# New priorities for the projections of the first attention pass, and a new table of scheduling rules, in a fused attention and token-MLP kernel

## The chip, the core and the metric

The kernel runs on one core of a Trainium2 chip. The metric is the device time of one execution in microseconds (us). The engines are PE (TensorE: matmuls; PEld is its weight load), DVE (VectorE), ACT (ScalarE), POOL (GpSimd) and SP (SyncE, which issues the DMAs).

## The reference

Two branches read the same normalised input, and the result joins them. B is 1, S is 2048, D is 640, there are 32 heads of 20, and F is 1536.

```python
xn = layernorm(x)                                   # over D
# A: attention
q, k, v = split_heads(xn @ wqkv)                    # 32 heads of 20
p = softmax(q @ k.T * 20**-0.5)                     # 2048 x 2048 for each head
s = merge_heads(p @ v) @ wo
# B: an MLP over the tokens
h = layernorm(xn)
u = gelu(einsum("bsd,sf->bdf", h, w1) + b1)         # tanh form
y = einsum("bdf,fs->bds", u, w2) + b2               # back to b, s, d
out = x + s * silu(y)
```

## The kernel before

**Units.** The heads are taken in eight groups G of four, and each group in passes of 512 queries. A pass has sixteen chunks of 128 keys. A *unit* is one chunk for one head and 512 queries: a PSUM bank of 128x512 scores. There are 2048 of them. A score matmul (line L1283) has 20 rows of real depth in a tile of 32 rows, so the four heads of a group run side by side in the array. The probabilities go into PV matmuls (L1381) that put the four heads side by side in columns, into one PSUM bank (bank 6), with a column of ones in V that sums the denominator. At the end of a pass (`ep_steps`) DVE transposes, divides and sends the result to DRAM.

**Two ways to an exponential.** ACT takes a *score group* of two or three PSUM banks (the groups are banks 0 to 2 and 3 to 5) and writes bf16 probabilities to `pt_sb` (L1313), a ring of 20 slots of 512. A slot is free again once its PV is done, and a group that doesn't fit at the ring's end starts over at slot 0. DVE instead makes an exponential out of bits: one operation writes the score as an integer that reads as a bf16 (L1324), and three operations on four units at a time (L1362) write copies of it that are shifted in the exponent's bits. PV adds the four versions, with V scaled for each (`vs_sb`, L766). So a DVE unit costs four PV matmuls where an ACT unit costs one. The scheduler lends DVE the third bank of an ACT group, and ACT then takes two.

**Other work.** The layer norm is on DVE and POOL. The first 512 rows of xn are transposed on PE, the others by DMA (`xTd_steps`, from `regC` to `xnT_sb`). For group 0, `qk_steps` makes q and k: five matmuls for 512 or 256 columns (L633), then one copy out of PSUM (by ACT at L1113/L1116, by DVE at L1114/L1117), scaled for q. `v_steps` with half 0 makes V of the first two groups, two chunks at a time: ten matmuls (L746), one copy. The projections of the later groups, the MLP (L648; L656 where a row of the array is used on its own) and the output projection (L965, L970) are cut into jobs that PE takes between the scores.

**The order.** No order is written out by hand. While the program is built, `schedule` plays the engines forward with costs of its own and fixes the order of each engine's instructions; on the chip each engine runs its list in order and waits on semaphores. The parts that the change touches are:

- Jobs that need a PSUM bank stand in `bankq`. During the *ramp* (until the tags in `RAMPEND` are done), `activate_` gives the next free bank (of 3, 4, 5 and 7 at first) to the job with the least of (time its first input is there, but not less than now + `KLEAD`; priority; place). Later it is the first that is due. A job holds its bank until its copy out of PSUM is done. During the ramp ACT and DVE both copy out; after it only DVE does.
- Priorities: 17 and 22.4 for the halves of q of the first block, `KPRIO` + block for keys, `VPRIO` + block for V, `QPRIO` for the second to fourth query blocks. A smaller number goes first. The scores of a pass need the query block of that pass (`qk0_0_1` is the second) and the chunk's keys (`qk0_1_3` is the last second half); PV needs the chunk's V.
- `pe_cands` offers PE the next score group, PV groups or a job's matmul, by ACT's deadline: the time at which ACT runs out of scores. If nothing is ready, and PE's recent activity is low, it sends a *filler* of four matmuls that add zeros into bank 6 (L1398; at the very start L1408). `SLACK`, `MINJ`, `ROOM`, `JOBF`, `LATE`, `PARTS`, `FGAP` are its thresholds. `LATE` is in passes, as are the due times.
- `do_st` decides whether DVE is lent a bank: `LEND` is the amount of work in DVE's queue above which it is not, `DRIDE` and `LONE` rule the extra bank 7. `D_GUARD` is the number of ACT units that must remain in a pass for DVE to take a chunk of it. `TOPP` and `EVP` are the priorities on DVE of the shifted copies and of copies out of PSUM.
- `MLP_A` and `MLP_B` spread the MLP's due times between these two passes. `OPM` is the number of 128-row blocks whose last 128 output columns share one bank and one product on DVE.
- `tune` is called every `WIN` = 16 claimed units and sets the options in `OPTS` to the values that one string of `PLAN` names, a digit for each option. `PLAN` is empty, so every option keeps its one value.

Of the kernel before, what the change touches and what calls it, by code (L numbers as in the profile page):

```python
# [265 lines left out]
class _Kern:  # L266
# [13 lines left out]
    AK = (1.0, 0.83984375, 0.70703125, 0.59375)  # L280
    MEAN4 = 4.159829600672171
    LOG2E = 1.4426950408889634
    D_GUARD = 16
    MLP_A, MLP_B = 2.6, 24.0
    QK_LEAD = 6.0
    SLACK, MINJ = 0.0, 640.0
    ROOM = 6
    ROWM, ROWP, ROWN = 5, 2, 400
    lastrow = None
    MERGE = False  # L290
    OPM = 2
    KLEAD = 300.0
    KPRIO = 22.4
    RAMPEND = ('qk0_1_3', 'qk0_0_1')
    RLEND = 0
    DRDY = 'xn15'
    OPR = 20.0
    QPRIO = (26.5, 29.0, 29.0)
    PVR = False
    JOBF = 4  # L300
    LONE, DLEAD, DRIDE = False, 0.0, 400.0
    NQS = 3
    CONFL = True
    FILL, FGAP, FACT = True, 0.0, 0.6
    LATE = 1.0
    LEND, LEND_MIN = 1800.0, 3
    SHARE = True
    VPRIO = 25.0
# [4 lines left out]
    QC = ((0.5, 3.0), (3.2, 6.4), (9.0, 13.5), (14.0, 18.0), (19.0, 22.0))  # L313
    WIN = 16
    DON = True
    TOPP, EVP = 38.0, 36.0
    GROT = 1
    OPTS = (
        ("SLACK", (120.0, 40.0, 200.0, 320.0)),
        ("MINJ", (640.0, 320.0, 1000.0)),  # L320
        ("ROOM", (3, 6, 0)),
        ("DRIDE", (400.0, 150.0, 700.0)),
        ("LEND", (1800.0, 1300.0, 2400.0, 700.0, 0.0)),
        ("PARTS", ((2,), (2, 1), (3, 1), (1,), ())),
        ("LATE", (2.0, -9.0, 99.0)),
        ("DON", (True, False)),
        ("LONE", (False, True)),
        ("CONFL", (True, False)),
        ("TOPP", (38.0, 22.0)),
        ("EVP", (24.0, 36.0)),  # L330
        ("FGAP", (40.0, 150.0)),
        ("GROT", (1, 0)),
    )
    PLAN = ()
    PARTS = (3, 1)
    DX = (1, 2, 3)
    V1A, V1B = 0.5, 4.0
# [73 lines left out]
    def schedule(self):  # L411
# [82 lines left out]
        def small(fn):  # L494
            def f(e):
# [6 lines left out]
               name="tl", cost=1400.0)  # L502
# [6 lines left out]
                name="id1", cost=300)  # L509
# [70 lines left out]
        def xtag(gb):  # L580
            return tuple(f"xTd{b}" for b in range(4 * gb, 4 * gb + 4)) if gb in DX else tuple(f"xT{gb}{h}_{d}" for h in ("a", "") for d in (0, 2, 4))
# [147 lines left out]
                     f"wp0_{w}", 430.0),  # L729
                    ("tag", f"wp0_{w}")]  # L730

        def v_steps(b, half):
            def make(bk):
                steps = []
                c0, n = (0, 160) if half == 0 else (160, 480)
                bl = [b] if half else [b, b + 1]
                for i, bb in enumerate(bl):
                    rd = [S_("wv")] + ([S_(f"xTb{bb}")] if bb // 4 in DX else [
                        S_(f"xT{dc}_0{'a' if bb < 2 else ''}") for dc in range(5)])
                    for dc in range(5):  # L740
# [5 lines left out]
                        steps.append(("pe", lambda e, dc=dc, i=i, bb=bb: e.matmul(  # L746
                            ps(bk, n, i * n), xnT_sb[:, dc, bb * 128:(bb + 1) * 128], wv_sb[:, dc, c0:c0 + n],
                            start=(dc == 0), stop=(dc == 4)), rd, [bank_slot[bk]], f"v{half}_{bb}", mm(n)))
# [271 lines left out]
        bankq = []  # L1020
# [6 lines left out]
            jobs.append(_Job(name, make if callable(make) else (lambda bk, m=make: m), requires, False, prio, at))  # L1027

        def add_bank_job(name, make, requires=(), prio=50.0, at=0.0):
            bankq.append(_Job(name, make, requires, True, prio, at))  # L1030

        def release(j):
            if j.bk is not None:
# [38 lines left out]
        def activate_():  # L1072
# [5 lines left out]
            while changed:  # L1078
# [493 lines left out]
        for gb in range(4):  # L1572
            if gb in DX:
                for b in range(4 * gb, 4 * gb + 4):
                    add_job(f"xTd{b}", xTd_steps(b), (f"xn{b}",), 22.0)
            xt = xtag(gb)
            if gb == 0:
                for h in (0, 1):
                    hp = "" if h else "a"
                    for dcs in ((0, 1), (2, 3), (4,)):  # L1580
                        add_bank_job(f"xT{h}_{dcs[0]}", xT_steps(h, dcs), (f"xn{2 * h}", f"xn{2 * h + 1}"), 18.0 + h)
                    xh = tuple(f"xT0{hp}_{d}" for d in (0, 2, 4))
                    add_bank_job(f"q0_0{hp}", qk_steps(0, 0, 256 * h, 256, hp), (f"xT0{hp}_0", "wp0_0"), 17.0 if h == 0 else 22.4)
# [24 lines left out]
        for G in range(1, NG):  # L1608
            cs = sorted({(80 * G - 80) // 128, (80 * G - 1) // 128})
            for w in (1, 0):  # L1610
# [5 lines left out]
                    at=(4 * G - 1.0 if G < NG - 1 else 24.0))  # L1616
# [484 lines left out]
        while True:  # L2101
# [84 lines left out]
```

## Time and profile before

| What | Value |
|---|---|
| Time, median of 3 runs | 753.57 us (753.44 to 754.69) |
| The profiled execution's own time | 754.1 us |
| Its span, first to last instruction | 752.3 us |
| Busy: PE, DVE, ACT | 716.3, 719.0, 730.0 us |
| Mean granted PE clock | 0.999 |
| Exps on ACT | 681 instructions, 1552 units |
| Exps on DVE | 496 units, 372 shifted copies |
| Filler matmuls (L1398) | 244 |
| DMA | 42.66 MB, 57 GB/s on the mean |

A line of the groups reads: source line, engine, operation, output <- inputs, shapes, count, then busy time and the mean duration of one in ns, then the idle time of the engine just before such instructions and what ended most of it. Durations of one engine's neighbours overlap, so the pace is read from the starts. A line of a timeline has the start and the duration in us, the operation, the count of merged instructions, and in brackets the idle time before it and its releaser. A line of the waits has the total, the number of times and the longest, in us.

### The profile page before, as it was taken

How to read it: one execution, taken by the hardware profiler on the slowest of the kernel's cores; microseconds unless marked ns; L12 is line 12 of the kernel's file. 1: busy time of each engine (PE TensorE's matmuls, PEld its weight loads, DVE VectorE, ACT ScalarE, POOL GpSimd, SP SyncE). 2: the span in 40 equal slices, each digit the busy share in tenths (PEclk: the TensorE clock that was granted, in tenths of full speed). 3: DMA queues.
4: the chain of work that ended last, by engine and by line, in shares of the span. 5: the costliest groups of instructions: out<-in, count | busy, mean ns of one | idle time of the engine just before them, and what ended most of it. 6: DMA issues, size and time to landing. Idle time of an engine off the chain costs nothing.

```text
span 752.3 us, 23672 instructions
## 1 busy us (share of the span) xinstructions
PE 716.3 (95%) x10561; PEld 243.6 (32%) x10561; DVE 719.0 (96%) x1320; ACT 730.0 (97%) x707; POOL 15.3 (2%) x23
## 2 busy tenths in 40 slices
PE   9899999999999999999999999999999999999997
PEld 7332222222233232323223332323233332333233
DVE  7889999999999999999999999999999999999996
ACT  5989999999999999999999999999999999999995
POOL 4200000000000000000000000000000000000000
PEclk9999999999999999999999999999999999999999
DMA  8754111110121031212111131301325501041102
GB/s 237 155 110 48 56 38 37 20 38 5 38 62 20 13 76 31 72 24 69 20 38 21 30 87 24 74 13 29 79 76 81 128 28 51 7 152 47 47 15 70
DMA packets 119738, 42.66 MB, mean 57 GB/s; under 512 B 79172, under 2 KB 118468, under 8 KB 119588
## 3 DMA queue, kind: packets, MB, share of 16 engines
q1 hardware_dynamic: 119636, 41.15, 23.4%
q8 instruction: 82, 1.34, 0.8%
q14 instruction: 20, 0.16, 0.1%
HBM read 26.37 MB, written 10.22 MB: 49 GB/s over the span
## 4 chain that ended last, share of the span: by engine, by line
ACT 76%; PE 18%; DVE 6%; issue 0%; DVEq 0%
ACT pt_sb L1313 74%; PE ps_all L1381 5%; PE ps_all L1283 5%; PE ps_all L648 5%; DVE dt_sb L1324 1%; PE ps_all L1408 1%; ACT zt_sb L849 1%; DVE dt_sb L1362 1%; ACT zt_sb L844 1%; DVE bst_sb L532 1%; DVE bst_sb L530 1%; DVE regC L548 1%; PE ps_all L965 1%; PE ps_all L633 0%; DVE v_sb L1114 0%; PE ps_all L746 0%
## 5 line engine op out<-in xcount | busy, mean ns | idle before, releaser
L1313 ACT ACTIVATE pt_sb<-ps_all 128x1024 bf16<-128x1024 f32 (+1 forms) x681 | 711.2, 1242 | 4.9 <-PE ps_all L1283 2.1
L1324 DVE TENSOR_SCALAR dt_sb<-ps_all 128x512 uint16<-128x512 f32 x496 | 328.4, 683 | 15.9 <-PE ps_all L1283 8.9
L1283 PE MATMUL ps_all<-qk_sb 32*128 32x512 bf16 (+1 forms) x2128 | 269.1, 376 | 26.4 <-ACT pt_sb L1313 22.9
L1362 DVE TENSOR_SCALAR dt_sb<-dt_sb 128x2048 uint16<-128x2048 uint16 x372 | 241.2, 689 | 1.5
L1283 PEld LDWEIGHTS ps_all<-qk_sb 32*128 32x128 bf16 x2128 | 68.4, 91 | 280.9 <-ACT pt_sb L1313 226.4
L1381 PE MATMUL ps_all<-dt_sb,vs_sb 128*21 128x512 bf16 (+1 forms) x1536 | 130.7, 376 | 0.9 <-DVE dt_sb L1362 0.5
L1381 PE MATMUL ps_all<-pt_sb,v_sb 128*21 128x512 bf16 (+1 forms) x1616 | 127.0, 374 | 1.9 <-DVE v_sb L1114 0.9
L648 PE MATMUL ps_all<-regC,regA 128*32 128x128 bf16 (+1 forms) x1472 | 65.5, 297 | 0.0
L648 PE MATMUL ps_all<-regB,regA 128*32 128x128 bf16 (+1 forms) x1480 | 65.2, 298 | 0.3 <-DVE qs_sb L698 0.3
L1381 PEld LDWEIGHTS ps_all<-dt_sb,vs_sb 128*21 128x21 bf16 x1536 | 33.4, 90 | 51.7 <-issue 31.2
L1381 PE MATMUL ps_all<-dt_sb,v_sb 128*21 128x512 bf16 (+1 forms) x512 | 49.2, 377 | 0.1
L1381 PEld LDWEIGHTS ps_all<-pt_sb,v_sb 128*21 128x21 bf16 x1616 | 30.9, 90 | 49.2 <-issue 35.9
L648 PE MATMUL ps_all<-xnT_sb,wqk_sb 128*32 128x512 bf16 x640 | 46.1, 382 | 0.0
L648 PEld LDWEIGHTS ps_all<-regB,regA 128*32 128x32 bf16 x1480 | 27.4, 96 | 23.3 <-issue 10.9
L648 PEld LDWEIGHTS ps_all<-regC,regA 128*32 128x32 bf16 x1472 | 27.8, 96 | 22.0 <-issue 10.6
L965 PE MATMUL ps_all<-wv_sb,xnT_sb 128*128 128x512 bf16 (+1 forms) x160 | 27.3, 301 | 0.0
L656 PE MATMUL ps_all<-regC,regA 32*128 32x512 bf16 x64 | 24.6, 384 | 0.0
L648 PE MATMUL ps_all<-wv_sb,xnT_sb 128*32 128x480 bf16 x320 | 22.1, 369 | 0.3 <-DVE qs_sb L1117 0.3
L1505 DVE STREAM_TRANSPOSE tr_sb<-ps_all 128x512 f32<-128x512 f32 x31 | 22.0, 711 | 0.0
L656 PE MATMUL ps_all<-regB,regA 32*128 32x512 bf16 x56 | 21.5, 384 | 0.0
L1381 PEld LDWEIGHTS ps_all<-dt_sb,v_sb 128*21 128x21 bf16 x512 | 13.0, 90 | 20.6 <-issue 14.2
L1398 PE MATMUL ps_all<-wp_sb,zw_sb 128*21 128x512 bf16 (+1 forms) x244 | 19.4, 373 | 0.0
(88 smaller groups left out, 348.5 us busy)
## 6 DMA issues: line engine op xcount, KB each, us to landing
regA<-in_B_w_dram SPq DMA_DIRECT2D x6, 1024.0 KB
regA<-in_B_w_dram SPq DMA_DIRECT2D x8, 768.0 KB
qk_sb<-qk_scratch_dram SPq DMA_DIRECT2D x56, 80.0 KB
qk_scratch_dram<-qs_sb SPq DMA_DIRECT2D x32, 128.0 KB
regA<-in_A_x_dram SPq DMA_DIRECT2D x6, 640.0 KB
ok_scratch_dram<-on_sb SPq DMA_DIRECT2D x96, 20.0 KB
out_dram<-regC SPq DMA_DIRECT2D x3, 640.0 KB
wqk_sb<-in_A_wqkv_dram SPq DMA_DIRECT2D x2, 480.0 KB
```

The lines of the kernel that those rows point to most:

```text
L530: steps.append(("dve", lambda e, b=b: e.bn_stats(bst_sb[:, b, 0:6], regA[:, b, 0:320]), [sx], [s0], f"{nm}s0", 393.0))
L532: steps.append(("dve", lambda e, b=b: e.bn_stats(bst_sb[:, b, 6:12], regA[:, b, 320:640]), [sx], [s1], f"{nm}s1", 393.0))
L648: fns.append(lambda e, c=c, e_=e_: e.matmul(oc(c, e_), lhsT[:, c:e_], rhs, start=start, stop=stop, tile_position=(0, c)))
L656: row = lambda g: (lambda e: e.matmul(oc(0, 128), lhsT[32 * g:32 * g + 32, :], rhs[32 * g:32 * g + 32, :], start=False, stop=False, tile_p ...
L965: steps.append(("pe", lambda e, c=c: e.matmul(ap, oT_sb[:, c, b * 128:(b + 1) * 128], wo_ap[:, c, c0:c0 + n], start=(opens and c == 0), st ...
L1283: t = pr.pe(lambda e, outp=outp, lhsT=lhsT, rhs=rhs, g=g: e.matmul(outp, lhsT, rhs, start=True, stop=True, tile_position=(32 * g, 0)), rea ...
L1313: tk = pr.act(lambda e: e.activation(outp, inp, AF.Exp, scale=math.log(2.0) / 128.0), reads=[bank_slot[b] for b in banks[:n]], writes=[S_( ...
L1324: tk = pr.dve(lambda e: e.tensor_scalar(w, src, WOFF, 0.0, ALU.add, ALU.max), reads=[bank_slot[bk]], writes=[S_(f"dt{d['tl'][0]}_{g}")], n ...
L1362: tk = pr.dve(lambda e: e.tensor_scalar(dst, src, dk, None, ALU.add), reads=[S_(f"dt{b}_{g}") for b in inb for g in range(4)], writes=[S_( ...
L1381: pr.pe(lambda e: e.matmul(outp, lhsT, rhs, start=(k == 0), stop=last, tile_position=(0, 32 * g)), reads=reads, writes=[bank_slot[AB]], na ...
L1398: pr.pe(lambda e, outp=outp, rhs=rhs, g=g: e.matmul(outp, zw_sb[:, 0:DH + 1], rhs, start=False, stop=False, tile_position=(0, 32 * g)), re ...
L1505: steps.append(("dve", lambda e: e.transpose(tr_sb[:, :], ps(AB)), [bank_slot[AB]], [S_("tr")], f"epT{q}", 632.0))
```

## The change

The jobs of the first pass that use a bank can get a priority of their own by name (`JP`). The V jobs are made from a list of groups (`VGRP`), which may have other sizes than two. The ramp ends without waiting for the second query block. Several fixed values change: `D_GUARD`, `MLP_B`, `OPM`, `KLEAD`, `LONE`, `DRIDE`, `LATE`, `EVP`. The options get some more values, `JOBF` becomes one of them, and `PLAN` has 128 strings, one for each 16 units; the first is applied before the first instruction is placed.

```diff
-    D_GUARD = 16
-    MLP_A, MLP_B = 2.6, 24.0
+    D_GUARD = 12
+    MLP_A, MLP_B = 2.6, 21.0
...
-    OPM = 2
-    KLEAD = 300.0
+    OPM = 4
+    KLEAD = 450.0
     KPRIO = 22.4
-    RAMPEND = ('qk0_1_3', 'qk0_0_1')
+    JP = {'q0_0': 26.0, 'k0_1a': 31.14, 'k0_2': 27.02, 'v0_11': 18.6, 'v0_3': 24.18, 'v0_10': 31.03, 'v0_13': 22.04, 'k0_0': 30.89, 'v0_0': 23.13}
+    VGRP = ((0, 2), (2, 2), (4, 2), (6, 2), (8, 2), (10, 2), (12, 2), (14, 2))
+    RAMPEND = ('qk0_1_3',)
...
-    LONE, DLEAD, DRIDE = False, 0.0, 400.0
+    LONE, DLEAD, DRIDE = True, 0.0, 250.0
...
-    LATE = 1.0
+    LATE = 2.0
...
-    TOPP, EVP = 38.0, 36.0
+    TOPP, EVP = 38.0, 18.0
...
     OPTS = (
-        ("SLACK", (120.0, 40.0, 200.0, 320.0)),
+        ("SLACK", (0.0, 120.0, 40.0, 200.0, 320.0)),
...
-        ("PARTS", ((2,), (2, 1), (3, 1), (1,), ())),
-        ("LATE", (2.0, -9.0, 99.0)),
+        ("PARTS", ((3, 1), (2,), (2, 1), (1,), ())),
+        ("LATE", (1.0, 2.0, -9.0, 99.0)),
...
-        ("EVP", (24.0, 36.0)),
-        ("FGAP", (40.0, 150.0)),
+        ("EVP", (36.0, 24.0)),
+        ("FGAP", (0.0, 40.0, 150.0)),
         ("GROT", (1, 0)),
+        ("JOBF", (4, 0, 8)),
     )
-    PLAN = ()
+    PLAN = (
+        "000000000000000", "000000000000000", "000000000000000", "000000000000000", "000000000000000", "200000000000000",
+        "000030000010000", "000000000000000", "000000000000000", "000000000000000", "000000000000000", "020000000000000",
...
+    )
...
-        def v_steps(b, half):
+        def v_steps(b, half, nb=2):
...
-                bl = [b] if half else [b, b + 1]
+                bl = [b] if half else list(range(b, b + nb))
...
-            bankq.append(_Job(name, make, requires, True, prio, at))
+            bankq.append(_Job(name, make, requires, True, self.JP.get(name, prio), at))
...
-            for b in range(4 * gb, 4 * gb + 4, 2):
-                add_bank_job(f"v0_{b}", v_steps(b, 0), xt + ((f"qk0_1_{gb}",) if gb else ("qk0_0_0", "qk0_1_0")), self.VPRIO + gb)
+            for b, nb in self.VGRP:
+                if (b + nb - 1) // 4 == gb:
+                    need = xt + (xtag(gb - 1) if b // 4 < gb else ())
+                    add_bank_job(f"v0_{b}", v_steps(b, 0, nb), need + ((f"qk0_1_{gb}",) if gb else ("qk0_0_0", "qk0_1_0")), self.VPRIO + gb)
```

More of the change, by code (lines that the diff above doesn't have):

```diff
@@ L315 @@
     DON = True
-    TOPP, EVP = 38.0, 36.0
+    TOPP, EVP = 38.0, 18.0
     GROT = 1
     OPTS = (
-        ("SLACK", (120.0, 40.0, 200.0, 320.0)),
+        ("SLACK", (0.0, 120.0, 40.0, 200.0, 320.0)),
         ("MINJ", (640.0, 320.0, 1000.0)),
-        ("ROOM", (3, 6, 0)),
+        ("ROOM", (6, 3, 0)),
         ("DRIDE", (400.0, 150.0, 700.0)),
         ("LEND", (1800.0, 1300.0, 2400.0, 700.0, 0.0)),
-        ("PARTS", ((2,), (2, 1), (3, 1), (1,), ())),
-        ("LATE", (2.0, -9.0, 99.0)),
+        ("PARTS", ((3, 1), (2,), (2, 1), (1,), ())),
+        ("LATE", (1.0, 2.0, -9.0, 99.0)),
         ("DON", (True, False)),
@@ L329 @@
         ("TOPP", (38.0, 22.0)),
-        ("EVP", (24.0, 36.0)),
-        ("FGAP", (40.0, 150.0)),
+        ("EVP", (36.0, 24.0)),
+        ("FGAP", (0.0, 40.0, 150.0)),
         ("GROT", (1, 0)),
+        ("JOBF", (4, 0, 8)),
     )
-    PLAN = ()
+    PLAN = (
+        "000000000000000", "000000000000000", "000000000000000", "000000000000000", "000000000000000", "200000000000000",
+        "000030000010000", "000000000000000", "000000000000000", "000000000000000", "000000000000000", "020000000000000",
+        "200000000000000", "000000000000002", "000000000000000", "010000000010000", "400000000000000", "000000000000000",
+        "001000000000001", "000000000000000", "000020000000000", "020000000000000", "200000000000000", "000000000000201",
+        "400000000000000", "010000000010000", "000004000000000", "000020000000000", "200000000000000", "000000000000000",
+        "000000000000000", "000000000000000", "000000000000000", "010000000010000", "000000000000000", "000000000000000",
+        "000030000010000", "020000000000000", "020004000000000", "010000000000000", "220020000000000", "000004000000000",
+        "000000000000000", "000000000000000", "010000000000000", "000030000010000", "000000000001000", "400000000000000",
+        "000020000000000", "200000000000000", "000000000000000", "000030000010000", "000030000000000", "000000000000000",
+        "000020000000000", "000000000000000", "000004000000200", "000020000000000", "010010000000000", "010010000000000",
+        "000102000010000", "000000000000000", "000020000000000", "000020000000000", "002000000000000", "001001000000000",
+        "020000000000000", "000000000000000", "000000000000000", "000000000000001", "000020000000000", "000020000000000",
+        "000000000000000", "000001000001000", "000000000000000", "000020000000000", "010000000010000", "000000000000000",
+        "010000000010000", "000020000000000", "000030000010000", "000000000000000", "200000000000000", "010004000010000",
+        "000000000000000", "000000000000000", "000000000000000", "000000000000000", "200000000000000", "200000000000000",
+        "000000000000000", "000000000000000", "000000000000000", "000010000000000", "000002000000000", "000000000000000",
+        "000000000000000", "000020000000000", "000004000000000", "000004000000000", "200000000000000", "000004000000000",
+        "000004000000000", "100000000000000", "000030000010000", "000030000010000", "000000000010000", "000004000000000",
+        "000030010000000", "000000000000000", "000004000000000", "000024000000000", "010000000010000", "000000000000000",
+        "000000000000000", "300000000010000", "000004000000000", "020000000000000", "010000000010000", "000000000000000",
+        "000000000000000", "000000000000200", "000030000010000", "010034000000000", "200000000000000", "000004000000000",
+        "000000000000000", "000030000010000",
+    )
```

## The prediction

> **What bounds the kernel now.** I read the page's shares first, then the groups by form, the chain of work, and the timelines of ACT and PE. From the page:
>
> ```profile
> span 752.3 us, 23672 instructions
> PE 716.3 (95%) x10561; PEld 243.6 (32%) x10561; DVE 719.0 (96%) x1320; ACT 730.0 (97%) x707; POOL 15.3 (2%) x23
> ACT 76%; PE 18%; DVE 6%; issue 0%; DVEq 0%
> ```
>
> Three engines are over 95% busy, but three quarters of the chain is ACT. The groups by form say with what:
>
> ```profile
> L1313 ACT ACTIVATE pt_sb<-ps_all 128x1024 bf16<-128x1024 f32 x491 | 481.3, 1127 | 0.9 <-PE ps_all L1283 0.5
> L1313 ACT ACTIVATE pt_sb<-ps_all 128x1536 bf16<-128x1536 f32 x190 | 285.9, 1541 | 4.0 <-PE ps_all L1381 1.9 <-PE ps_all L1283 1.7
> L1324 DVE TENSOR_SCALAR dt_sb<-ps_all 128x512 uint16<-128x512 f32 x496 | 328.4, 683 | 15.9 <-PE ps_all L1283 8.9 <-PE ps_all L656 5.7
> L1362 DVE TENSOR_SCALAR dt_sb<-dt_sb 128x2048 uint16<-128x2048 uint16 x372 | 241.2, 689 | 1.5
> L1398 PE MATMUL ps_all<-wp_sb,zw_sb 128*21 128x512 bf16 x224 | 18.5, 382 | 0.0
> ```
>
> All 2048 score units are here: 491×2 + 190×3 = 1552 on ACT and 496 on DVE. The mean of 1127 ns is not a pace, since successive exps overlap: in the timeline most start 0.904 us apart (two banks) or 1.331 us (three), the fourteen tanh 1.16 us. So ACT's own work is 491×0.904 + 190×1.331 + 14×1.16 = 713.0 us. The first exp starts at 12.09 us, the last ends at 743.59: 731.5 us. Of the 18.5 us between, 1.5 are projections copied out by ACT; 17.0 us are waiting. The starts put 5.4 us of it before 42 us and 11.6 us after. Of the 11.6, 6.9 us are 31 waits of over 0.1 us, scattered from 70 to 726 us, the rest small change. Most of that hides in the overlap and never shows in the idle column. What lies outside the exps is 12.1 us ahead and 8.7 us behind.
>
> The ramp's waiting is in ACT's timeline:
>
> ```profile
> 14.73 2.79 ACT L1313 ACTIVATE pt_sb<-ps_all 128x1536 bf16<-128x1536 f32 x2 [0.78 <-PE ps_all L1283]
> ...
> 21.30 6.82 ACT L1313 ACTIVATE pt_sb<-ps_all 128x1536 bf16<-128x1536 f32 x5 [0.49 <-PE ps_all L1283]
> 28.33 8.18 ACT L1313 ACTIVATE pt_sb<-ps_all 128x1536 bf16<-128x1536 f32 x6 [0.20 <-PE ps_all L1283]
> 37.46 0.60 ACT L1116 ACTIVATE qk_sb<-ps_all 128x512 bf16<-128x512 f32 x1 [0.95 <-PE ps_all L633]
> ```
>
> Sixteen exps of three units pass; then ACT waits 0.95 us for the second query block and 1.93 us more. All engines' timeline shows what for:
>
> ```profile
> 38.11 0.87 PE L746 MATMUL ps_all<-wv_sb,xnT_sb 128*128 128x160 bf16 x10 [0.69 <-ACT qk_sb L1116]
> 38.91 0.40 PE L1398 MATMUL ps_all<-wp_sb,zw_sb 128*21 128x512 bf16 x4
> 39.02 0.49 DVE L1114 CAST v_sb<-ps_all 128x320 bf16<-128x320 f32 x1
> 39.56 0.61 PE L1381 MATMUL ps_all<-pt_sb,v_sb 128*21 128x512 bf16 x8 [0.26 <-DVE v_sb L1114]
> 39.99 9.81 ACT L1313 ACTIVATE pt_sb<-ps_all 128x1536 bf16<-128x1536 f32 x9 [1.93 <-PE ps_all L1381]
> ```
>
> The scores of exp 17 were ready (L1283 at 35.22 us). It waited for room in `pt_sb`, whose 20 slots hold six groups of three. A group leaves by PV (L1381), which lacked V; V's matmul lacked the bank that the query block held until ACT had copied it out. So the first pass ends on: query block, bank, V, PV, exp.
>
> **The change part by part.**
>
> *Projections of the first pass.* The instruction order of the changed kernel puts the second query block (five matmuls of 512) five score groups earlier, ahead of the last three key halves, with DVE copying it out. Three V blocks stand between key halves, where there were two. `VGRP` has the old pairs, and `v0_3`, `v0_11`, `v0_13` name no job: these move nothing. The early q costs PE 5×0.216 = 1.1 us, and the fills of 33 to 35 us (three groups, 0.65 us) show where it goes; if that cover is missing, one key half is 1.1 us later. On DVE the copy (0.60 us) stands behind the layer norm and ahead of a key's; the scores of those keys wait behind it. ACT copies six q/k blocks of 256 (0.33 us each) instead of four and one of 512 (0.55): 0.1 us more.
>
> ACT after: twelve exps run on from 21.3 us, 12×1.331 = 16.0, with the 0.37 us that stands before 28.33, then one key copy of 0.33 us: exp 18 at 38.0 us. Before it was 39.99 + 1.33 = 41.3. Gain 3.3 us if nothing new is late; 2.4 if the key copy waits as the q copy did (0.95); 1.4 if the PV wait (1.93) returns, which is the bound against it. I take 2.6, nearer to the free case: in the order, the PV that exp 17 lacked now stands ahead of score group 18 instead of behind it, and its V no longer behind the query block's bank. All three engines begin the steady part that much earlier, since DVE's first exp (42.57 us) waits for the same end of the ramp.
>
> *Units.* DVE gets 492 instead of 496, ACT 490 exps of two and 192 of three. ACT: −0.904 + 2×1.331 = **+1.8 us**, all on the bounding engine. DVE drops 4×0.60 + 3×0.60 = 4.2 us, which is not the bound.
>
> *The table.* Every sixteen units it sets when DVE is lent a bank, how far PE runs into ACT's deadline, and how many copies PV takes. The first string also overrides the new values of `LONE`, `DRIDE`, `LATE` and `EVP` with the old ones, so those edits move nothing. The table adds no instruction; its whole effect is on the 11.6 us. Evidence from the order: filler groups of four (L1398) fall from 61 to 39; in the first 128 units from 15 to 11, so 18 of the 22 go later. A filler is sent only when PE has nothing else, so PE is starved some 18×0.22 = 4 us less. Against it, PE changes between tilings 1306 times for 1292 (a run of eight PV takes 0.54 us after scores, 0.43 without a change, so 0.11 each: +1.5 us). From below, the gain cannot pass the 6.9 us of waits over 0.1 us; from the other side, the denser rows of now show what can be lost: 0.97 us of waiting in 600:620 against 0.1 to 0.3 in quiet rows, a loss of 3 us if four or five more rows become like it. I take **−3.0**, nearer to the filler count than to either end.
>
> *MLP due by pass 21 instead of 24.* No work is added. Between units 640 and 768 PE's matmuls, at 0.216 us per slot, rise from 33.5 to 36.1 us; between 1536 and 1792 they fall from 74.5 to 71.3. ACT paces 128 units at about 45 us, so PE fits before and after: zero, inside the table's bounds. `OPM` 4 makes eight narrow products (0.28 us) into three wide (0.60) and two narrow, 0.2 us on DVE, covered by its 3.38 us idle before the tail. The tail's order from the last PV on is the old one: 0 ± 0.3.
>
> *Fillers and the clock.* The granted clock is 1.00 in every 20 us row up to 740, and the longest wait that PE's loads show is short:
>
> ```profile
> PEld ps_all L1283 <- ACT pt_sb L1313: 226.4, 512, 1.2
> ```
>
> A rule speaks against dropping fillers: the Trainium skill, "TensorE: Matmul & The Clock Gate", Part 1, says that an idle window of about 3.4 us halves the array's clock, and that a busy one is needed to restore it. An estimate from its figures is 1.7 us for each such event, so the sum by it would be 1.7 us worse for one. With 1.2 us as the longest wait I charge nothing by the row.
>
> **Sum.** −2.6 (ramp) + 1.8 (units) − 3.0 (table) + 0 (tail) = −3.8 us. The profiled execution took 754.1 us (span 752.3 and 1.8 around it): 750.3 after. It was 0.5 us above the median of 753.57, so I predict **749.8 us**. About 0.2%, 1.5 us, can be told from no change here.
>
> **The rivals.**
>
> - *The ramp alone pays.* The table trades large waits for small ones, and PE's 1.5 us of changes eat the fillers' time: −2.6 + 1.8 = −0.8, or 752.8 us. For it: 4.7 of the 11.6 us are already small. Against: 18 filler groups gone. 0.14.
> - *Dense PE turns the sign.* With the MLP due earlier, out of units 640 to 1152 (180 us, nine rows) score groups arrive late as in 600:620. At 0.97 us per row instead of about 0.3 that is +6.0; with −2.6 and +1.8, 758.8 us. It decides, that is slows the kernel, once more than 0.8 us is lost in those rows. For it: the largest 128-unit sum grows from 37.9 to 38.2 us. Against: 38 is far under 45. 0.12; a small share of it gives 755.
> - *All large waits go.* −3.3 + 1.8 − 6.9 = −8.4, or 745.2 us. For it: a choice every sixteen units can address each wait. Against: DVE and PE have no long free stretch either. 0.11.
>
> The main case has 0.63. Its own range, with the ramp at 1.4 to 3.3 and the table at 0 to −6, reaches 746 to 754. Range 745.8 to 754.5 for 8 in 10. Faster by over 0.2% (under 752.1): 0.74, nearly all of the main case and the third rival. Within: 0.13. Slower (over 755.1): 0.13.
>
> **What would show it.** Right: exp 18 starts at 38 to 39 us, without the 1.93 us wait on L1381; 490 and 192 exps; waits over 0.1 us on ACT after 42 us sum to 3 to 5 us; clock 1.00. Wrong in the ramp: a wait of over 1 us for L1381 or L633 before 42 us. Wrong in the table: ACT's waiting after the ramp stays at 11 us or more, most of it between 240 and 430 us if the MLP is the reason. Wrong in the units: another pace than 0.904 and 1.331.

## The result and the profile after

The changed kernel takes 751.3 us (median of 7 runs, 751.0 to 751.43); the kernel before took 753.6 us beside it (7 runs, 753.42 to 754.69). The ratio is 0.9967, with a 95% interval of 0.9955 to 0.9978. The profiled execution took 751.3 us, its span 749.5 us; the granted clock is 1.0. The forecast was 749.8 us.

Lines of code that the schedule touches stand 26 further down (L1313 is now L1339, L1283 is L1309, L1381 is L1407, L1398 is L1424, L633 is L659). From the page of the changed kernel:

```profile
span 749.5 us, 23450 instructions
PE 710.4 (95%) x10453; PEld 240.2 (32%) x10453; DVE 716.3 (96%) x1309; ACT 730.8 (98%) x709; POOL 15.4 (2%) x23
ACT 89%; PE 9%; DVE 2%; DMA 0%; issue 0%
```

ACT's share of the chain rose from 76% to 89%: it is the bound more clearly than before. The groups by form of the changed kernel (count, then busy time and mean duration in ns):

```profile
L1339 ACT ACTIVATE pt_sb<-ps_all 128x1024 bf16<-128x1024 f32 x490 | 480.4, 1146 | 0.5
L1350 DVE TENSOR_SCALAR dt_sb<-ps_all 128x512 uint16<-128x512 f32 x492 | 324.3, 680 | 16.7 <-PE ps_all L1309 10.5 <-PE ps_all L682 4.0
L1339 ACT ACTIVATE pt_sb<-ps_all 128x1536 bf16<-128x1536 f32 x192 | 288.2, 1560 | 2.0 <-PE ps_all L1309 1.6
...
L1424 PE MATMUL ps_all<-wp_sb,zw_sb 128*21 128x512 bf16 x152 | 13.0, 383 | 0.0
```

490 and 192 exps, 492 units on DVE, and 152 wide fillers where there were 224: the counts of instructions are those that the order showed. The ramp in ACT's timeline:

```profile
14.58 2.79 ACT L1339 ACTIVATE pt_sb<-ps_all 128x1536 bf16<-128x1536 f32 x2 [0.98 <-PE ps_all L1309]
...
21.34 16.40 ACT L1339 ACTIVATE pt_sb<-ps_all 128x1536 bf16<-128x1536 f32 x12 [0.67 <-PE ps_all L1309]
37.59 0.42 ACT L1139 ACTIVATE qk_sb<-ps_all 128x256 bf16<-128x256 f32 x1
37.86 9.26 ACT L1339 ACTIVATE pt_sb<-ps_all 128x1536 bf16<-128x1536 f32 x9
```

Twelve exps run on without a gap, a key block is copied, and exp 18 starts at 37.86 us, where it started at 41.33. Neither the 0.95 us wait for the query block nor the 1.93 us wait for PV is left. The timeline of all engines shows why:

```profile
28.54 1.25 PE L659 MATMUL ps_all<-xnT_sb,wp_sb 128*128 128x512 bf16 x5
...
29.83 0.69 DVE L1143 TENSOR_SCALAR qk_sb<-ps_all 128x512 bf16<-128x512 f32 x1
...
34.38 0.73 PE L772 MATMUL ps_all<-wv_sb,xnT_sb 128*128 128x160 bf16 x8
...
35.15 0.49 DVE L1140 CAST v_sb<-ps_all 128x320 bf16<-128x320 f32 x1
...
35.69 0.61 PE L1407 MATMUL ps_all<-pt_sb,v_sb 128*21 128x512 bf16 x8
```

The second query block is computed at 28.5 us and copied by DVE at 29.8; V is ready at 35.6, and the PV that frees slots of `pt_sb` runs at 35.69 us. Before, V's matmul began at 38.11 and that PV at 39.56 us.

With each exp at its pace (0.904 or 1.331 us, tanh 1.16, a copy 0.33 us, or 0.55 us for 512 columns), what is left between the starts on ACT is waiting. In us:

| | Before | After | Difference |
|---|---|---|---|
| First exp starts | 12.09 | 11.60 | -0.5 |
| Waiting before 42 us | 5.1 | 2.0 | -3.1 |
| Copies by ACT | 1.5 | 1.6 | +0.1 |
| Work of exps and tanh | 713.0 | 714.7 | +1.8 |
| Waiting after 42 us | 11.6 | 10.3 | -1.35 |
| of it in waits over 0.1 us | 6.9 (31) | 6.3 (35) | -0.7 |
| Behind the last exp (tail) | 8.7 | 9.0 | +0.3 |
| Span | 752.3 | 749.5 | -2.8 |

In both columns the terms come to some 0.3 us less than the span, since the last exp lasts longer than its pace; the 5.4 us that the forecast names for the waiting before 42 us has this in it. The first line is no effect of the change: the instructions up to there stand in the same order, and over the kernels below the first exp starts anywhere from 10.99 to 12.01 us. By 21.3 us the two kernels are level (21.30 and 21.34 us), and from there to exp 18 it is 20.0 us before and 16.5 us after. In the profiles of the other kernels with the new priorities exp 18 starts between 37.4 and 38.8 us, so the gain in the ramp is known to about a microsecond. The spans differ by 0.5 us more than the medians (2.3 us), because the profiled execution of the kernel before, at 754.1 us, was 0.5 us above its median; where these 0.5 us lie is not shown.

### The profile page after: what moved, and what is told of

Same layout as the page of the kernel before. It is cut to its first block, busy times and chain, and to the rows that moved or that the text cites. A ratio compares the mean times of both kernels' runs of the same rounds, so it can differ in the third digit from the quotient of the medians.

```text
span 749.5 us, 23450 instructions
## 1 busy us (share of the span) xinstructions
PE 710.4 (95%) x10453; PEld 240.2 (32%) x10453; DVE 716.3 (96%) x1309; ACT 730.8 (98%) x709; POOL 15.4 (2%) x23
## 4 chain that ended last, share of the span: by engine, by line
ACT 89%; PE 9%; DVE 2%; DMA 0%; issue 0%
ACT pt_sb L1339 87%; PE ps_all L1309 2%; PE ps_all L1407 2%; PE ps_all L674 2%; ACT zt_sb L875 1%; PE ps_all L1434 1%; ACT zt_sb L870 1%; PE ps_all L991 1%; DMA xnT_sb<-regC 0%; PE ps_all L659 0%; DVE bst_sb L558 0%; DVE bst_sb L556 0%; DVE regC L574 0%; DVE regC L1747 0%; PE ps_all L717 0%
## 5 line engine op out<-in xcount | busy, mean ns | idle before, releaser
L1339 ACT ACTIVATE pt_sb<-ps_all 128x1024 bf16<-128x1024 f32 (+1 forms) x682 | 712.9, 1263 | 2.4 <-PE ps_all L1309 1.6
L1350 DVE TENSOR_SCALAR dt_sb<-ps_all 128x512 uint16<-128x512 f32 x492 | 324.3, 680 | 16.7 <-PE ps_all L1309 10.5
L1309 PE MATMUL ps_all<-qk_sb 32*128 32x512 bf16 (+1 forms) x2128 | 268.7, 376 | 29.5 <-ACT pt_sb L1339 26.5
L1388 DVE TENSOR_SCALAR dt_sb<-dt_sb 128x2048 uint16<-128x2048 uint16 x369 | 238.7, 682 | 1.2
L1309 PEld LDWEIGHTS ps_all<-qk_sb 32*128 32x128 bf16 x2128 | 67.9, 91 | 284.7 <-ACT pt_sb L1339 234.6
L1407 PE MATMUL ps_all<-pt_sb,v_sb 128*21 128x512 bf16 (+1 forms) x1624 | 125.3, 374 | 0.9 <-DVE v_sb L1140 0.3
L1407 PE MATMUL ps_all<-dt_sb,vs_sb 128*21 128x512 bf16 (+1 forms) x1512 | 124.4, 377 | 0.5 <-DVE dt_sb L1388 0.4
L1407 PE MATMUL ps_all<-dt_sb,v_sb 128*21 128x512 bf16 (+1 forms) x504 | 48.9, 379 | 0.4 <-DVE tr_sb L1523 0.2
L1407 PEld LDWEIGHTS ps_all<-dt_sb,vs_sb 128*21 128x21 bf16 x1512 | 33.0, 91 | 45.4 <-issue 26.9
L1407 PEld LDWEIGHTS ps_all<-pt_sb,v_sb 128*21 128x21 bf16 x1624 | 28.7, 90 | 47.8 <-issue 39.3
L674 PEld LDWEIGHTS ps_all<-regB,regA 128*32 128x32 bf16 x1484 | 27.5, 96 | 24.6 <-issue 12.2
L682 PE MATMUL ps_all<-regC,regA 32*128 32x512 bf16 x76 | 29.2, 384 | 0.0
L991 PE MATMUL ps_all<-wv_sb,xnT_sb 128*128 128x512 bf16 (+1 forms) x160 | 27.5, 301 | 0.1
L682 PE MATMUL ps_all<-regB,regA 32*128 32x512 bf16 x52 | 20.0, 385 | 0.0
L1407 PEld LDWEIGHTS ps_all<-dt_sb,v_sb 128*21 128x21 bf16 x504 | 12.9, 90 | 21.6 <-issue 15.8
L674 PEld LDWEIGHTS ps_all<-xnT_sb,wqk_sb 128*32 128x32 bf16 x640 | 13.7, 95 | 18.0 <-issue 10.4
```

What stands on the lines that cost most here:

```text
L674: fns.append(lambda e, c=c, e_=e_: e.matmul(oc(c, e_), lhsT[:, c:e_], rhs, start=start, stop=stop, tile_position=(0, c)))
L682: row = lambda g: (lambda e: e.matmul(oc(0, 128), lhsT[32 * g:32 * g + 32, :], rhs[32 * g:32 * g + 32, :], start=False, stop=False, tile_p ...
L991: steps.append(("pe", lambda e, c=c: e.matmul(ap, oT_sb[:, c, b * 128:(b + 1) * 128], wo_ap[:, c, c0:c0 + n], start=(opens and c == 0), st ...
L1309: t = pr.pe(lambda e, outp=outp, lhsT=lhsT, rhs=rhs, g=g: e.matmul(outp, lhsT, rhs, start=True, stop=True, tile_position=(32 * g, 0)), rea ...
L1339: tk = pr.act(lambda e: e.activation(outp, inp, AF.Exp, scale=math.log(2.0) / 128.0), reads=[bank_slot[b] for b in banks[:n]], writes=[S_( ...
L1350: tk = pr.dve(lambda e: e.tensor_scalar(w, src, WOFF, 0.0, ALU.add, ALU.max), reads=[bank_slot[bk]], writes=[S_(f"dt{d['tl'][0]}_{g}")], n ...
```

## The experiments

Times of the kernel before are 753.8 to 754.1 us beside these runs. "Waiting" is ACT's waiting after 42 us, reckoned as above; the tail is from the end of the last exp to the end of the span. The units on DVE are counted in the profile.

| Run | Median us | Ratio, 95% | DVE units | Waiting | Tail |
|---|---|---|---|---|---|
| The changed kernel | 751.3 | 0.9967 [0.9955, 0.9978] | 492 | 10.3 | 9.0 |
| e1_priorities_alone | 774.29 | 1.0264 [1.0249, 1.0279] | 492 | 13.3 | 28.0 |
| e2_no_table | 759.72 | 1.0077 [1.0056, 1.0099] | 488 | 17.5 | 10.1 |
| e3_half_table | 751.84 | 0.997 [0.996, 0.998] | 496 | 12.6 | 9.0 |
| e4_ring_of_21 | 771.36 | 1.0227 [1.0214, 1.0241] | 500 | 11.0 | 28.0 |
| e5_thin_fillers_after | 753.05 | 0.9988 [0.9975, 1.0002] | 492 | 11.6 | 8.7 |
| e6_thin_fillers_before | 755.3 | 1.0019 [1.0005, 1.0033] | 496 | 13.3 | 8.7 |
| e7_guard_16 | 762.5 | 1.0115 [1.01, 1.013] | 492 | 14.3 | 15.7 |
| e8_table_of_92 | 755.07 | 1.0016 [1.0007, 1.0024] | 500 | 11.1 | 15.1 |
| e9_table_of_116 | 751.23 | 0.9968 [0.9956, 0.9981] | 496 | 11.1 | 10.1 |
| e10_table_of_122 | 755.65 | 1.0025 [1.0015, 1.0034] | 496 | 10.1 | 15.1 |
| e11_priorities_guard_12 | 763.03 | 1.0128 [1.0115, 1.0142] | 492 | 13.1 | 17.6 |
| e12_priorities_mlp_21 | 761.08 | 1.0099 [1.0084, 1.0115] | 480 | 13.1 | 10.1 |

### The priorities alone

The kernel before with the new priorities, and no table and no other value of the change.

```diff
-    KLEAD = 300.0
+    KLEAD = 450.0
-    RAMPEND = ('qk0_1_3', 'qk0_0_1')
+    JP = {'q0_0': 26.0, 'k0_1a': 31.14, 'k0_2': 27.02, 'v0_11': 18.6, 'v0_3': 24.18, 'v0_10': 31.03, 'v0_13': 22.04, 'k0_0': 30.89, 'v0_0': 23.13}
+    RAMPEND = ('qk0_1_3',)
...
-            bankq.append(_Job(name, make, requires, True, prio, at))
+            bankq.append(_Job(name, make, requires, True, self.JP.get(name, prio), at))
```

> The kernel before, with the new priorities by name, KLEAD 450 and the shorter RAMPEND alone: no table, MLP_B 24, OPM 2, D_GUARD 16. By its order ACT gets 491 exps of two banks, 191 of three, one of one (DVE 492 units): 1.8 us more ACT work than before. Theory A (time = ramp + ACT's work + its waits, and the priorities act in the ramp alone): exp 18 starts at 37.9 us without the wait of 1.93 us, waits after 42 us stay at 11 to 12 us, so -3.1 + 1.8 = -1.3: about 752.3 us. Theory B (the ramp is given back later, as DVE and PE are no earlier): exp 18 early, but waits after 42 us up by 2 to 3 us, about 754.5 us.

The ramp did what the forecast says, if 0.9 us late: exp 18 at 38.83 us, the waiting before 42 us 2.9 instead of 5.1 us. Its instruction order in the ramp is that of the changed kernel, so the 1.0 us between their exps 18 is variation between executions. The waiting after 42 us is 13.3 us, of which 2.3 lie where the clock granted to PE fell to a half for 6.83 us, at 653.0 us (more on this under the fillers' width). Yet the kernel lost 20 us, which neither theory had, and nearly all of it in the tail, which grew from 8.7 to 28.0 us. Up to the last exp it is only 0.9 us behind the kernel before: that exp ends at 744.5 us, where it ended at 743.6. PE's timeline in the tail of this run (start, duration, operation, count, idle time and its releaser):

```profile
753.38 1.25 PE L966 MATMUL ps_all<-wv_sb,xnT_sb 128*128 128x512 bf16 x5 [0.79 <-DVE regC L981]
755.42 0.73 PE L966 MATMUL ps_all<-wv_sb,xnT_sb 128*128 128x128 bf16 x10 [0.79 <-DVE regC L981]
756.67 1.25 PE L966 MATMUL ps_all<-wv_sb,xnT_sb 128*128 128x512 bf16 x5 [0.52 <-DVE regC L995]
758.70 1.25 PE L966 MATMUL ps_all<-wv_sb,xnT_sb 128*128 128x512 bf16 x5 [0.79 <-DVE regC L981]
```

It is the output projection: 110 of its 160 matmuls stand behind the last scores (31 in the kernel before). Five matmuls of 512 take 1.25 us, then PE waits 0.79 us for DVE to take the product out of its bank. In the same order of instructions the MLP's last matmul comes at unit 1963 of 2048, where the kernel before has it at 1832. The chain is seen in the DMA issues: `regA`, which holds the MLP's weights, is loaded again with x for the output, here late,

```profile
711.27 3.01 SPq L1657 DMA_DIRECT2D regA<-in_A_x_dram  x4
```

and early in the kernel before (first) and in the changed kernel (second):

```profile
665.36 2.45 SPq L1656 DMA_DIRECT2D regA<-in_A_x_dram  x4
```

```profile
660.37 2.70 SPq L1684 DMA_DIRECT2D regA<-in_A_x_dram  x4
```

### A longer ring instead

The kernel before with 21 slots in `pt_sb`, so that a seventh group of three fits while V is late; statistics of the layer norm share places to make room.

```diff
-    RP = 20
+    RP = 21
...
-            sb("bst_sb", [P, NB, 12], f32)
-            sb("st_sb", [P, 8, NB], f32)
+            sb("bst_sb", [P, 8, 12], f32)
+            sb("st_sb", [P, 7, NB], f32)
```

> The kernel before with 21 slots in pt_sb instead of 20, so that seven groups of three fit and not six; room is made by letting the statistics of the layer norm share eight rows. With 20 slots this gives the order of before. DVE gets 500 units, ACT 501 exps of two and 182 of three: 1.7 us less ACT work. Theory A (exp 17 waited for room in the ring): the wait of 1.93 us on L1381 at 38 us is gone or under 0.5 us, exp 18 at 39.5 us or earlier, 753.6 - 1.9 - 1.7: about 750 us. Rival E (exp 17 waited for the second query block and V, whatever the ring): a wait of 1.5 us or more stays before 42 us, 752 us.

ACT's timeline shows what became of the wait:

```profile
28.02 9.52 ACT L1313 ACTIVATE pt_sb<-ps_all 128x1536 bf16<-128x1536 f32 x7 [0.20 <-PE ps_all L1283]
...
40.27 2.36 ACT L1313 ACTIVATE pt_sb<-ps_all 128x1536 bf16<-128x1536 f32 x2 [2.25 <-PE ps_all L1381]
```

Exp 17 passes, and exp 18 waits for the same PV, 2.25 us instead of 1.93. Exp 18 starts at 40.28 us, 1.06 us earlier than before, of which 0.5 us is an earlier first exp. Theory A had the wait gone and exp 18 at 39.5 us or earlier; it failed, and Rival E, with a wait of 1.5 us or more, held. So one more place moves the wait by one exp, while the new priorities, with an earlier V, remove it: the late query block and V were the cause, as the chain of the forecast has it. The median is 771.36 us where the theories had 750 and 752: the tail, which neither had, is 28.0 us again, and again the output projection starts late (706.6 us).

### The two values that hold the tail

D_GUARD back to 16 in the changed kernel, and to 12 or the MLP's due time to 21 in the kernel with the priorities alone.

```diff
# e7, in the changed kernel
-    D_GUARD = 12
+    D_GUARD = 16
# e11, in e1
-    D_GUARD = 16
+    D_GUARD = 12
# e12, in e1
-    MLP_A, MLP_B = 2.6, 24.0
+    MLP_A, MLP_B = 2.6, 21.0
```

> The changed kernel with D_GUARD 16 instead of 12, table kept. ACT's work is the same (490 and 192 exps), but by its order the MLP's last matmul comes at unit 1886 instead of 1821, and 62 output-projection matmuls instead of 35 stand behind the last score. Theory T (what is left of the output projection when the attention ends sets the tail: 110 and 100 such matmuls gave 28 us, 31 and 35 gave 8.7 and 9.0, so 0.25 us each): tail 15 to 17 us, about 758 us. Theory A (ramp, ACT's work and ACT's waits are all): 751 to 752 us.

> The kernel before with the new priorities and D_GUARD 12, nothing else: DVE 492 units, and the MLP's last matmul is placed at unit 1878, where the priorities alone have 1963 and the kernel before 1832; 57 matmuls of the output projection stand behind the last scores, against 110 and 31. Theory T (the tail is the output projection that a late MLP pushes behind the scores): tail 14 to 16 us against 28 with the priorities alone, median 760 to 763. Theory N (the tail comes from the new priorities in another way): tail stays at 26 us or more, median 772 to 775.

> The kernel before with the new priorities and the MLP due by pass 21, nothing else: the MLP's last matmul at unit 1868, 40 matmuls of the output projection behind the last scores, but DVE gets only 480 units, so ACT has 6.8 us more exps than before. Theory T: tail 9 to 11 us, and the median is 754.1 - 3.0 (ramp) + 6.8 (units) + 1 (tail) = 758.9 us (756 to 761, less if DVE's lighter load saves waiting). Theory N: tail 26 us or more, median 774 or more.

| Kernel | Last MLP matmul starts | Output projection starts | Last exp ends | Room | Tail |
|---|---|---|---|---|---|
| Before | 665.1 | 668.4 | 743.6 | 75.2 | 8.7 |
| After | 657.2 | 668.4 | 740.5 | 72.1 | 9.0 |
| e12 | 680.7 | 686.3 | 748.3 | 62.0 | 10.1 |
| e7 | 683.5 | 688.1 | 744.6 | 56.5 | 15.7 |
| e11 | 681.5 | 689.1 | 743.4 | 54.3 | 17.6 |
| e4 | 696.6 | 706.6 | 740.6 | 34.0 | 28.0 |
| e1 | 711.0 | 717.0 | 744.5 | 27.5 | 28.0 |

(us; room is what lies between the start of the output projection and the end of the last exp.) The tail follows the room: nothing is lost with 72 us, little with 62, 7 to 9 us with 54 to 57, 19 us with 34 or less. Room is not all that makes a tail: the tables of 92 and 122, with 70 us of room, have 15.1 us for another reason, given below. e7 was forecast well in the tail (15 to 17), but its total is 4 us above what the tail makes, since ACT also waits 4 us more. e11's tail missed its range by 1.6 us. e12's tail came as forecast; its total, 761.08 us, was just above the range, since its waiting is 1.5 us above that of before instead of equal, and a single wait of 1.5 us stands at a halved clock there (591 us). Each of the two values shortens the tail by itself, from 28.0 to 17.6 or 10.1 us; the earlier due time also takes 12 units off DVE (480 for 492), which ACT then does. Why the new priorities of the first 40 us put the MLP's end 130 units later in the schedule is inside the builder's own play of the engines and was not traced.

### The table

Without it, with its first half, with its first 92, 116 and 122 strings of 128. The other strings are all zeros; in the kernel without a table the old LONE, DRIDE, LATE and EVP stand as values.

```diff
# e2, in the changed kernel
-    LONE, DLEAD, DRIDE = True, 0.0, 250.0
+    LONE, DLEAD, DRIDE = False, 0.0, 400.0
-    LATE = 2.0
+    LATE = 1.0
-    TOPP, EVP = 38.0, 18.0
+    TOPP, EVP = 38.0, 36.0
-    PLAN = (
...
+    PLAN = ()
# e3, e8; in e9 and e10 likewise the last 12 and 6 strings
-        "000000000000000", "300000000010000", "000004000000000", "020000000000000", "010000000010000", "000000000000000",
...
+        "000000000000000", "000000000000000", "000000000000000", "000000000000000", "000000000000000", "000000000000000",
...
```

> The changed kernel with an empty PLAN and the options' old fixed values, all else as changed (D_GUARD 12, MLP_B 21, OPM 4, new ramp). DVE gets 488 units, ACT 489 exps of two and 194 of three: 3.5 us more ACT work than before, 1.8 more than with the table. Theory A (the table is worth its four DVE units and little of the waiting): waits after 42 us 10 to 12 us, 753 to 754 us. Theory C (the table is there for the waits, the units are incidental): waits after 42 us rise by 3 us or more over those with the table (10.3), 755 us or more.

> The changed kernel with the first 64 strings of PLAN and zeros for the other 64. DVE gets 496 units, ACT 495 exps of two, 187 of three and one of one: ACT work as before the change (+0.1 us). Theory A (units rule): 1.7 us less than with the whole table, waits alike: 749.5 us. Theory D (the table's gain is in its second half, where the waits of 300 to 400 and 500 to 700 us fell from 6.1 to 3.9 us): these waits return, 751.3 - 1.7 + 2.3: 752 us or more.

> The changed kernel with the first 92 strings of the table and zeros for the other 36. DVE gets 500 units, ACT 495 exps of two and 186 of three: 3.5 us less ACT work than with the whole table; 35 output-projection matmuls behind the last score, as with the whole table. Theory A (units): 748 us if ACT waits as now. Theory C (the table is there for the waits and the clock): with 36 strings at zero, waits rise by 3 us or more or the clock drops, 751 us or more.

> The changed kernel with the first 116 strings of the table, the last 12 all zeros. Up to unit 1856 the instructions stand as in the changed kernel; from there DVE gets four more units (496), which takes 1.8 us of exps off ACT, and the last four-unit group of DVE ends before the last scores, as in the changed kernel. Theory L (the long tail of the table of 92 is DVE's last group of four, dealt behind all scores): the tail is 9 us, the median 749.5 us (748.5 to 750.5), the last unit of DVE starts before 735 us. Theory W (each string zeroed loses waiting, wherever it stands): waiting after 42 us grows by 2 us or more and the median is 751 to 753. A version that beats both kernels, if L holds.

> The changed kernel with the first 122 strings, the last 6 all zeros: also 496 units on DVE, and the same ACT work as with 116 strings, with fewer strings zeroed. In its instruction order the last two scores of a group of DVE stand behind the output projection's matmuls, and PV behind them in four separate runs of eight, as with the table of 92. Theory L: the tail is 15 us instead of 9, the last unit of DVE starts about 11 us before the end of the span, and the median is 755 us (753.5 to 757). Theory W: at least as fast as the table of 116, 749 to 751 us, tail 9.

The table is worth 8.4 us of the median: 759.72 without it, 751.3 with it. In the spans that is 10.1 us: 7.2 of waiting, 1.8 of exps (488 units on DVE for 492), 1.1 of tail. Of the 7.2 us, 3.7 lie at two stretches in which the granted clock was halved (449 and 565 us). The times agree: the one execution of e2 with a mean clock of 1.0 took 757.46 us, 6.2 us more than with the table, the three of 0.993 or less 761.2 to 762.8 us. So a part of the table's worth is that the clock stays up. Its first half keeps nearly all of the whole: e3 waits 2.3 us more, of which 1.4 at such a stretch (445 us), but has four more units on DVE. Its three executions at a clock of 1.0 took 750.6 to 750.8 us, the eight at 0.998 from 751.5 to 753.4 us. Theory D, by which the waits of the second half come back, comes near the total (752 us or more) for the wrong reason: between 500 and 700 us e3 waits 3.0 us, the changed kernel 2.8.

The tables of 92, 116 and 122 are about the end. The first two of the next three fences show DVE's own exps from 720 us on (count, shortest, median and longest in ns, first and last start) in the changed kernel and in the table of 116, the third in the table of 122:

```profile
L1350 DVE TENSOR_SCALAR dt_sb<-ps_all x10: 640/680/693, 719.5 to 732.4; 128x512 uint16<-128x512 f32 x10
```

```profile
L1350 DVE TENSOR_SCALAR dt_sb<-ps_all x12: 652/681/693, 720.1 to 734.2; 128x512 uint16<-128x512 f32 x12
```

```profile
L1350 DVE TENSOR_SCALAR dt_sb<-ps_all x12: 642/680/693, 721.8 to 743.7; 128x512 uint16<-128x512 f32 x12
```

With 122 strings DVE's last unit starts at 743.7 us, behind the last exp (738.8), and its three shifted copies and four runs of PV follow one after another: the tail is 15.1 us. With 116 strings it starts at 734.2 and the tail is 10.1. ACT's exps are the same amount in both, the waiting 10.1 and 11.1 us: that one late group costs 4.4 us of the median. The table of 92 has the same end and the same tail, which its expectation had not seen. The table of 116 was to beat both kernels by the 1.8 us of exps that it takes off ACT; it gave 1.1 back in the tail and 0.8 in waiting and is equal to the changed kernel. No version run here has a median that is faster than the changed one beyond the noise; the half table comes to 0.6 us less only in its executions at full clock.

### The fillers' width

Both kernels with their order unchanged, but each filler matmul adds 32 columns instead of 512 or 256.

```diff
-                outp = ps_all[32 * g:32 * g + DH + 1, AB * 512 + a:AB * 512 + a + n]
-                rhs = wp_sb[:, 0:n // 256, :, :]
+                outp = ps_all[32 * g:32 * g + DH + 1, AB * 512 + a:AB * 512 + a + 32]
+                rhs = wp_sb[:, 0, 0, 0:32]
```

> The changed kernel, instruction for instruction in the same order on every engine, but each filler matmul (L1424) is 32 columns wide instead of 512 or 256: the places are kept, the array's work in them goes. Theory F (the fillers hold the granted clock; the half clock seen for 3.4 to 6.8 us in two of the kernels without the table, or with half of it, comes where PE's work is thin): one or more stretches at half clock after 40 us, each +2 to +4 us of ACT waiting, 753 to 760 us. Theory N (39 groups of fillers are idle time with another name): clock 1.00, 751.3 us within 0.3.

> The kernel before with its 61 groups of fillers thinned to 32 columns in the same way, order unchanged. Theory F: more such stretches than in the changed kernel with thin fillers, since it has 22 groups more to lose: 756 us or more. Theory N: 753.6 us within 0.3.

With thin fillers the granted clock halves for 6.83 us at 565.4 us in the changed kernel, and for 3.41 us at 359.0 and again at 516.0 in the kernel before. The table by windows of the changed kernel with thin fillers (us, then busy us of PE, PEld, DVE, ACT, POOL, the clock, the DMA share, GB/s):

```profile
562.00:565.40 3.40, 2.41 (x33) 0.71 (x32) 3.40 (x7) 3.40 (x5) 0.00 (x0) 1.00 0.34 38
565.40:572.30 6.90, 6.78 (x63) 1.58 (x67) 5.81 (x11) 6.76 (x8) 0.00 (x0) 0.51 0.70 107
```

and what ACT meets there:

```profile
574.22 1.94 ACT L1339 ACTIVATE pt_sb<-ps_all 128x1024 bf16<-128x1024 f32 x2 [1.00 <-PE ps_all L682]
```

Waiting rises by 1.3 us (after) and 1.7 us (before) with the same instructions otherwise, nearly all in the hundreds of us with the half clock. The medians follow with 1.7 and about 1.3 us, but the executions spread widely, and the mean clock of each tells why. In the changed kernel the three with 0.999 or 1.0 took 750.4 to 751.5 us, as with full width, the nine with 0.995 or less 751.9 to 756.6 us. In the kernel before the five with 0.999 or 1.0 took 753.9 to 754.4 us, the seven below that 755.2 to 760.0 us. So the thin fillers cost nothing but the half clock, and how often that comes differs between executions. Theory F has the mechanism; but the kernel before, with 22 groups more to thin, lost no more than the changed one, and its 755.3 us lies below the 756 that Theory F gave. Fillers of full width are thus worth one to two us in either kernel. With wide fillers the half clock shows up too, where PE is thinly fed: in the kernel without the table,

```profile
568.47 1.45 ACT L1316 ACTIVATE pt_sb<-ps_all 128x1536 bf16<-128x1536 f32 x1 [1.02 <-PE ps_all L1286]
570.83 6.20 ACT L1316 ACTIVATE pt_sb<-ps_all 128x1536 bf16<-128x1536 f32 x5 [0.91 <-PE ps_all L1286]
```

stand in a stretch from 565.4 to 572.2 us at a clock of 0.5. The priorities alone, the half table and the priorities with the earlier MLP have such a stretch too, at 653.0, 444.6 and 591.0 us; the profiles of the kernel before and the changed kernel have none ahead of the tail. (Of 59 executions of the kernel before beside these runs two had a mean clock of 0.998; they took 756.0 and 756.2 us.) With the priorities alone, two rows of the windows and two lines of PE's timeline there read:

```profile
650.00:653.00 3.00, 1.78 (x20) 0.49 (x17) 3.00 (x7) 3.00 (x4) 0.00 (x0) 1.00 0.00 0
653.00:660.00 7.00, 6.57 (x51) 1.32 (x48) 4.62 (x10) 5.23 (x6) 0.00 (x0) 0.51 0.06 20
```

```profile
651.92 0.39 PE L1284 MATMUL ps_all<-qk_sb 32*128 32x512 bf16 x3 [0.53 <-ACT pt_sb L1314]
...
653.75 0.61 PE L1284 MATMUL ps_all<-qk_sb 32*128 32x512 bf16 x3 [0.43 <-ACT pt_sb L1314]
```

## Why the prediction was right, and where it was not

**The ramp: right.** Forecast exp 18 at 38.0 us, taken as 2.6 us of gain after a discount; measured 37.86 us, 3.1 us less waiting and 0.1 us more copying. The discount for the key copy was not needed: DVE's copy of the query block and the earlier V leave no wait before the copy. The reason holds by three runs: the early query block and V remove the wait with no table (e1, e2), and more ring does not (e4). In the instruction order, `KLEAD` alone, `RAMPEND` on top of the other two and the entries that name no job change no instruction. With the named priorities, though, `KLEAD` 450 for 300 does change the order, from ACT's tenth exp on. So within the ramp it is the named priorities and `KLEAD` together that act, and no run has one without the other.

**The units: right.** +1.8 us of exps on ACT, 490 and 192, at the paces of before.

**The table: mis-sized.** The term was -3.0 us and measured -1.35. The step that failed is "PE is starved some 18×0.22 = 4 us less": the count of fillers does not tell how long ACT waits. Without the table there are 42 filler groups, fewer than the 61 of before, and ACT waits 17.5 us (13.8 without the 3.7 at half clock); with the table there are 39, and it waits 10.3. The term was also one number for two things of opposite sign. The other edits raise the waiting from 11.6 to 17.5 us, and the table takes 7.2 off, about half of it by keeping the clock up, which the forecast had priced at nothing. Which of the other edits raises the waiting is not shown. Waits over 0.1 us fell to 6.3 us, not to the 3 to 5 that were to show the term right; but the total stayed below the 11 that were to show it wrong. The third rival (all large waits go) is refuted by the same number. The first rival (the ramp alone pays, 752.8 us) is half true: the measured 751.3 lies midway between it and the forecast.

**The MLP's due time: zero, but not for the reason given.** The forecast said that PE fits before and after, and costed `D_GUARD` at nothing without a word. With the priorities both decide when the MLP ends and so whether the output projection fits beside the exps: D_GUARD 16 would have cost 11.2 us (e7: 6.7 of tail, 4.0 of waiting), and neither value, with no table, 23 us (e1). A cover was named for PE's work in the middle of the kernel; the one that counted was the 72 us of exps beside the output projection. The forecast's zero came out since it read in the changed kernel's instructions that the tail's order is the old one (35 matmuls of the output projection behind the last scores for 31). What holds the tail there it did not see; that both far-off values were already set right for it is luck.

**Dense PE (the slower rival): refuted.** It needed more than 0.8 us of loss between 240 and 430 us. There the waiting rose by 0.3 us, from 3.0 to 3.3 us. The slower end that did lie near was another one, the late MLP.

**The clock: right here, by a cover.** The Trainium skill, "TensorE: Matmul & The Clock Gate", Part 1, has the clock halve after an idle window of about 3.4 us. The lengths agree: 3.41 us or twice that, in every case. The idleness does not: before the half clock at 565.4 us PE was busy for 2.41 of 3.40 us, and before that at 653.0 in the run of the priorities alone the longest single wait of a matmul is 0.53 us. The changed kernel has one of 0.95 us (at 267.7 us) and keeps its clock. So the longest wait, 1.2 us, on which the forecast charged nothing, is no proof of safety, and here the measurement decides. The cost in ACT's waiting, against the same stretch of a kernel without it, is 0.7 to 1.5 us for 3.41 us of half clock and 1.6 to 2.3 us for 6.83; the estimate from the rule was 1.7 us for each event.

## What to carry to other kernels

If an engine waits for a slot, look for what frees the slot before adding slots: here one more place moved the wait by one exp, while an earlier producer removed it. When a list scheduler is given another start, read in its order how much of the last phase stands behind the bounding engine's last instruction; a gain of 3 us at the start cost 19 us at the end until two far-off values were set anew. Price a set of rules by the kernel without it, not by a by-product such as the number of fillers, and compare executions of the same clock.

## What the hardware showed that was not expected

The granted clock fell to a half without any long idle time on PE: with matmuls busy for 2.41 of 3.40 us (thin fillers, 565.4 us) or 1.78 of 3.00 us (priorities alone, 653.0 us) and no wait over 0.6 us it halved for 6.83 us, and a matmul group that took 0.39 us took 0.61. Whether a filler holds the clock depends on its width: 512 columns did in the profiles of both kernels, 32 columns in the same places did not, and 16 of the 24 executions with them had a mean clock below 0.999.
